# Chunked attention into a swish layer: compact q and k, 64x64 products, v in 128-token rows, stores from ScalarE's queue

## The chip, the cores and the metric

The kernel runs on one core of one Trainium2 chip. The metric is the device time of one execution in microseconds (us); lower is better. All medians and ratios below are of fast runs; a run over 1.5% above the fastest of its kernel counts as slow and is left out. The profile is a trace of one execution, with its own span (the kernel before: 403.8 us).

A core has five engines here, each with its own in-order stream of instructions: TensorE (PE in the profile; PEld are its weight loads), ScalarE (ACT), VectorE (DVE), GpSimd (POOL) and SyncE (SP), which only starts DMAs. A name with a trailing q (SPq, ACTq) is an engine's sequencer at work on issuing a DMA. An issue by ScalarE stands in ScalarE's own stream, between its computations.

## The reference, cut to what matters

```python
# q, k, v: (B=8, H=8, S=576, D=64); softmax only within chunks of 64 tokens
scores = 0.125 * q_chunk @ k_chunk.T          # 64 x 64 for each head and chunk
attn   = exp(scores - max) / sum
x      = (attn @ v_chunk)  -> (B*S = 4608 tokens, H*D = 512)
h      = x @ w_in                             # (4608, 512) @ (512, 2048)
g      = h * sigmoid(beta * h)
out    = g @ w_out                            # (4608, 2048) @ (2048, 512), float32
```

All inputs and the output are float32; the kernels compute in bfloat16. The sigmoid is done as a tanh: g is (tanh(beta h / 2) + 1) * h, and the factor 0.5 is applied when the result is stored. The maximum is left out of the softmax, and the sum comes from a column of ones beside v.

## The kernel before

The tokens are worked in nine blocks of 512. Blocks 0 to 7 are the first 512 tokens of each batch. Block 8 ("LAST") holds the 64 tokens that are left of each of the eight batches, so its q and k come in 32 DMAs of 64 KB instead of 8 of 256 KB. A block has two halves `h` of 256 tokens.

The program is a list of events with planned times. They are sorted by time and each is appended to the streams of its engines; semaphores are placed by a helper. The planned time has no other meaning than this order. From block 3 on, TensorE alternates a group of four 512-column products of the first layer (`mm1`, block b) with one of the second layer (`mm2`, block b-1), and the attention of block b+1 is strewn between them:

```python
        def load_v(blk, hb, halves, queue):          # 8 issues a block, 64 partitions each
            ...
                        a = v[blk][4 * hb + hp, 64 * c0:64 * c1, :].rearrange("(c k) d -> k c d", k=64)
            ...
                    return e.dma_start(vstage[64 * hb:64 * hb + 64, s, hp, c0:c1, :], a)

        def widen_k(h, hb, eng):                     # k into block-diagonal form, on GpSimd
            ...
                copy(eng, kBD[r, s, hp, :, 64 * hb:64 * hb + 64].rearrange("k c (t i) -> k c t i", t=8),
                     qkT[r, s, 1, :, :].rearrange("k i (c t h) -> k h c t i", c=4, h=4)[:, hp], ...)

        def gate(blk, t, n, halves=(0, 1)):          # tanh on ScalarE, g on VectorE
            ...

        def store(blk, s, n, cols=(0, 512), eng="act", queues=("sp", "sp")):
            ...                                      # evict PSUM on ScalarE, then two DMAs of 128 KB

        def rest(h, tc, tx, tk, t0, step, tX, tv):   # attention of half h
            for w in range(2):
                at(tc + 1.05 * w, cast_qk, h, w, "pool")
            at(tx, turn_dma, h)                      # DMA transpose of q and k, issued by SyncE
            for hb in range(2):
                at(tk + 2.0 * hb, widen_k, h, hb, "pool")
            at(tv, cast_v, h, "pool")
            for u in range(2):
                at(t0 + step * u, scores, ...)
                at(t0 + step * u + 0.3, exp, ...)
                at(t0 + step * (u + 1.5), attend, ...)
                at(t0 + step * (u + 1.5) + 0.3, normalize, ...)
            at(tX, turn_x_dma, h)                    # DMA transpose of x, issued by SyncE

        for blk in range(3, NB):
            b = begin(blk)
            for h in (2 * blk, 2 * blk + 1):
                for which in range(2):
                    at(b - 34, load_qk, h, which, "sp")
            for hb in range(2):
                at(b - 33.5, load_v, blk, hb, (0, 1), "sp")
            rest(2 * blk, b - 27, b - 24.5, b - 20.5, b - 15, 1.74, b - 9.5, b - 17)
            rest(2 * blk + 1, b - 24, b - 21.5, b - 15.5, b - 10, 1.74, b - 4.5, b - 12)
```

SyncE thus issues, in one order: q and k loads, v loads, the two q/k transposes, the two x transposes, and the stores in between. An issue whose data is not ready stops all that stand behind it.

## Time and profile before

| | kernel before |
|---|---|
| median of the three fast runs (range) | 402.83 us (401.52 to 405.39; a fourth, of 407.59, was slow) |
| span of the trace | 403.8 us |
| TensorE busy | 308.0 us (76%) |
| mean granted TensorE clock | 0.915 of full |

These are lines of the page of the kernel before. The rows of digits cut the span into 40 slices of about 10 us: a digit is the busy share in tenths, and in the row PEclk the granted clock. The line of the chain gives shares of the span by engine. The groups give line, engine, operation, shapes and count, then busy us, mean ns of one, and idle time just before with what ended most of it.

```profile
PE 308.0 (76%) x2020; PEld 158.9 (39%) x2049; DVE 145.0 (36%) x257; ACT 168.8 (42%) x275; POOL 130.4 (32%) x191
...
PE   1688986895698896898489938993899305899996
...
PEclk9999998898889998999699968998899855999999
...
PE 47%; SPq 18%; DMA 13%; DVE 7%; POOL 5%; ACT 5%; issue 4%; POOLq 0%; ACTq 0%
...
L381 PE MATMUL A<-qkT,kBD 128*128 128x64 bf16 x224 | 18.7, 235 | 49.5 <-POOL kBD L215 49.5
```

No engine is full. In the row PE a hole comes back about every four slices from the twentieth on, and the clock drops in the same place. In the chain of work that ended last, SyncE's queue (SPq) and DMAs make up 31%. The scores' products on TensorE (the last line) waited 49.5 us in all for the widened k.

The time line of SyncE between two blocks shows why the widened k is late. Columns: start us, duration us, engine, line, operation, destination and source, number of issues.

```profile
172.54 1.23 SPq L445 DMA_TRANSPOSE xT<-xn  x1
173.82 1.27 SPq L259 DMA_DIRECT2D qkstage<-in_q_dram  x2
...
179.00 8.11 SPq L281 DMA_DIRECT2D vstage<-in_v_dram  x8
187.16 1.34 SPq L510 DMA_DIRECT2D out_dram<-ostage  x2
188.54 3.32 SPq L347 DMA_TRANSPOSE qkT<-qkb  x1
...
193.17 3.15 SPq L347 DMA_TRANSPOSE qkT<-qkb  x1
...
213.63 1.23 SPq L445 DMA_TRANSPOSE xT<-xn  x1
```

And this is TensorE in that stretch; the bracket tells how long it was idle before the line, and who released it:

```profile
189.53 1.03 PE L460 MATMUL F<-xT,w_in_bf 128*128 128x512 bf16 x4
196.49 0.39 PE L381 MATMUL A<-qkT,kBD 128*128 128x64 bf16 x4 [5.93 <-POOL kBD L215]
...
197.68 1.49 PE L491 MATMUL F<-w_out_bf,g 128*128 128x512 bf16 x3 [0.22 <-issue]
```

A block is a loop: the second x transpose of one block leaves (172.54), only then do the next block's q and k loads, its v loads (8.11 us) and a store go out, then the q/k transpose (188.54); GpSimd widens k, the scores start (196.49, 24 us after the x transpose), and 17 us later the next second x transpose leaves (213.63). Together that is 41 us. TensorE stood for 5.93 us, and its next products ran at about half speed (three in 1.49 us against 0.81 at the full clock).

### The profile page before, as it was taken

To read this page: it belongs to the slowest core of one execution; us is meant where nothing else is said; L and a number is where in the kernel's file an instruction comes from. 1 tells how busy PE (TensorE), PEld (TensorE's weight loads), DVE (VectorE), ACT (ScalarE), POOL (GpSimd) and SP (SyncE) were. 2 spreads that over 40 slices of the span, in tenths; PEclk is the share of its full clock that TensorE was granted. 3 is DMA by queue.
4 is the path that set the end of the run, shared out by engine and by line. 5 is a ranking of instruction groups with operands and counts; after the bars stand their busy time and mean duration, and the time that the engine had idled before them with its cause. 6 is when DMAs were issued, how large, how long until landed. Compare 5 with 4: busy or idle time off the path is not lost.

```text
span 403.8 us, 5337 instructions
## 1 busy us (share of the span) xinstructions
PE 308.0 (76%) x2020; PEld 158.9 (39%) x2049; DVE 145.0 (36%) x257; ACT 168.8 (42%) x275; POOL 130.4 (32%) x191
## 2 busy tenths in 40 slices
PE   1688986895698896898489938993899305899996
PEld 1553444562344332433244414441444102444444
DVE  5257424551127531543044403541254200444410
ACT  1656235564147452535254515442454202545421
POOL 2544342417760128222831364034601218200000
PEclk9999998898889998999699968998899855999999
DMA  9997997992822695179516970699053295130112
GB/s 195 312 341 289 291 254 171 211 191 67 155 54 54 195 189 111 42 230 171 130 32 200 194 148 2 164 222 165 23 93 94 94 177 117 26 80 26 52 54 78
DMA packets 102809, 57.51 MB, mean 142 GB/s; under 512 B 84208, under 2 KB 85504, under 8 KB 102784
## 3 DMA queue, kind: packets, MB, share of 16 engines
q1 hardware_dynamic: 100432, 56.51, 61.1%
q10 hardware_dynamic: 2352, 0.66, 0.9%
q8 instruction: 16, 0.26, 0.3%
q14 instruction: 9, 0.07, 0.1%
HBM read 36.71 MB, written 9.44 MB: 114 GB/s over the span
## 4 chain that ended last, share of the span: by engine, by line
PE 47%; SPq 18%; DMA 13%; DVE 7%; POOL 5%; ACT 5%; issue 4%; POOLq 0%; ACTq 0%
PE F L491 20%; PE F L460 17%; DMA qkT<-qkb 8%; SPq L281 7%; SPq L267 5%; POOL kBD L215 5%; SPq L259 4%; DVE g L478 4%; PE A L381 3%; ACT tt L475 3%; PE A L414 3%; DMA xT<-xn 3%; PE A L460 2%; DVE xn L429 2%; SPq L510 2%
## 5 line engine op out<-in xcount | busy, mean ns | idle before, releaser
L478 DVE SCALAR_TENSOR_TENSOR g<-tt,F 128x512 bf16<-128x512 bf16 (+1 forms) x148 | 92.3, 629 | 201.5 <-ACT tt L475 201.2
L460 PE MATMUL F<-xT,w_in_bf 128*128 128x512 bf16 (+1 forms) x608 | 142.2, 368 | 14.7 <-DMA xT<-xn 7.7
L491 PE MATMUL F<-w_out_bf,g 128*128 128x512 bf16 (+1 forms) x563 | 146.8, 390 | 2.9 <-issue 0.8
L475 ACT ACTIVATE tt<-F,beta_half 128x512 bf16<-128x512 f32 (+1 forms) x148 | 93.5, 641 | 117.7 <-PE F L460 116.6
L460 PEld LDWEIGHTS F<-xT,w_in_bf 128*128 128x128 bf16 x608 | 59.0, 102 | 71.7 <-issue 10.2
L215 POOL COPY kBD<-qkT 64x256 bf16<-64x256 bf16 x112 | 64.7, 619 | 64.2 <-DMA qkT<-qkb 63.0
L491 PEld LDWEIGHTS F<-w_out_bf,g 128*128 128x128 bf16 x592 | 57.9, 101 | 63.3 <-issue 6.6
L215 POOL CAST qkb<-qkstage 128x1024 bf16<-128x1024 f32 x32 | 33.1, 1039 | 125.0 <-DMA qkstage<-in_q_dram 86.6
L381 PE MATMUL A<-qkT,kBD 128*128 128x64 bf16 x224 | 18.7, 235 | 49.5 <-POOL kBD L215 49.5
L398 ACT ACTIVATE EBD<-A 64x512 bf16<-64x512 f32 x56 | 32.9, 587 | 55.9 <-PE A L381 55.2
L381 PEld LDWEIGHTS A<-qkT,kBD 128*128 128x128 bf16 x224 | 15.0, 115 | 60.0 <-POOL kBD L215 55.1
L209 ACT ACTIVATE ostage<-F 128x512 f32<-128x512 f32 (+1 forms) x36 | 21.3, 591 | 26.6 <-PE F L491 20.6
L429 DVE TENSOR_TENSOR xn<-A,R 128x512 bf16<-128x512 f32 x36 | 24.9, 691 | 1.2
L215 POOL CAST v_bf<-vstage 128x1024 bf16<-128x1024 f32 x18 | 18.7, 1036 | 12.9 <-DMA vstage<-in_v_dram 12.0
L414 PE MATMUL A<-v_bf,EBD 128*128 128x65 bf16 x224 | 12.2, 198 | 8.9 <-DVE xn L429 8.4
L414 PEld LDWEIGHTS A<-v_bf,EBD 128*128 128x128 bf16 x224 | 10.8, 101 | 18.3 <-DVE xn L429 12.6
L427 DVE RECIPROCAL R<-A 128x8 f32<-128x8 f32 x36 | 7.3, 202 | 26.1 <-PE A L414 25.7
L460 PE MATMUL A<-xT,w_in_bf 128*128 128x512 bf16 x48 | 11.2, 380 | 2.4 <-DVE w_in_bf L215 1.3
L325 PE MATMUL F<-ident,qkb 128*128 128x128 bf16 x32 | 4.2, 312 | 8.2 <-DVE qkb L215 6.3
L475 ACT ACTIVATE tt<-A,beta_half 128x512 bf16<-128x512 f32 x12 | 8.2, 687 | 4.2 <-PE A L460 4.2
L478 DVE SCALAR_TENSOR_TENSOR g<-tt,A 128x512 bf16<-128x512 bf16 x12 | 8.2, 686 | 2.9 <-ACT tt L475 2.9
L215 POOL CAST w_in_bf<-wstage 128x512 bf16<-128x512 f32 x12 | 7.0, 615 | 6.3 <-DMA wstage<-in_moe_w_in_dram 6.3
(40 smaller groups left out, 74.2 us busy)
## 6 DMA issues: line engine op xcount, KB each, us to landing
out_dram<-ostage SPq DMA_DIRECT2D x70, 128.0 KB
qkstage<-in_q_dram SPq DMA_DIRECT2D x32, 256.0 KB, 3.4
qkstage<-in_k_dram SPq DMA_DIRECT2D x32, 256.0 KB, 5.4
vstage<-in_v_dram SPq DMA_DIRECT2D x56, 128.0 KB, 4.2
wstage<-in_moe_w_out_dram SPq DMA_DIRECT2D x4, 1024.0 KB
wstage<-in_moe_w_in_dram SPq DMA_DIRECT2D x3, 1024.0 KB
vstage<-in_v_dram SPq DMA_DIRECT2D x24, 64.0 KB, 5.4
wstage<-in_moe_w_in_dram SPq DMA_DIRECT2D x2, 512.0 KB
```

Source lines behind the costliest of these rows:

```text
L209: P.op("act", lambda e: e.activation(dst, src, AF.Copy, **kw), reads, writes)
L215: P.op(eng, lambda e: e.tensor_copy(dst, src), reads, writes, rows)
L267: return e.dma_start(qkstage[32 * c:32 * c + 32, s, which, hb, :], src[4 * hv + c][heads, S - 64:S, :].rearrange("h (t i) d -> t h (i d)", ...
L281: return e.dma_start(vstage[64 * hb:64 * hb + 64, s, hp, c0:c1, :], a)
L381: return e.matmul(unit_out(n, i, 64, r).rearrange("k (i t) -> k i t", i=8), kk, q_of(h, r, c, hp))
L398: P.op("act", lambda e, r=r: e.activation(EBD[r, s, u, :, r.start:r.stop], bank(n)[r, :].rearrange("p (x q) -> p x q", q=64), AF.Exp, scal ...
L414: return e.matmul(unit_out(banks[hp2], c, 65, r), ee, v_bf[r, sv, 2 * u + hp2, 4 * hv + c, 0:65])
L429: P.op("dve", lambda e: e.tensor_tensor(xn[:, s, :, u, :].rearrange("p c (b d) -> p b c d", b=2), o[:, :, :, 0:64], R[:, u, :, :].unsqueez ...
L460: return e.matmul(bank(n)[:, 64 * c0:64 * c1].rearrange("p (c t) -> p c t", t=64), w_in_bf[:, kt, 128 * t:128 * t + 128], xT[:, sx, c0:c1, ...
L475: P.op("act", lambda e: e.activation(tt[:, T % 3, c], bank(n)[:, c], AF.Tanh, scale=beta_half[:, t:t + 1]), reads=[K("ps", n, v=("h", blk, ...
L478: P.op("dve", lambda e: e.scalar_tensor_tensor(g2[:, sg, t, c], tt[:, T % 3, c], 1.0, bank(n)[:, c], ALU.add, ALU.mult), reads=[K("ps", n, ...
L491: P.op("pe", lambda e, t=t: e.matmul(bank(n)[:, 0:b - a], g2[:, sg, t, 128 * s:128 * s + 128], w_out_bf[:, t, a:b], start=(t == 0), stop=( ...
```

## The change

The intent is to make attention cheaper on every engine beside TensorE and to shorten SyncE's queue. q and k are put in token order once by GpSimd ("order"), so that neither a block-diagonal k nor zeroes are needed; scores and attention times v become 64x64 products on the four quarter tiles of TensorE; exp is one instruction for a half; v is loaded with 128 tokens on the partitions, in 4 issues a block instead of 8, half of them behind the q/k transposes; ScalarE issues the stores; w_out is loaded in runs of 4 KB (and beta, w_in columns and stored rows are rearranged to fit); q and k have a fourth buffer.

```diff
-        NQ = 3
+        NQ = 4
...
-        def load_v(blk, hb, halves, queue):
...
+        def load_v(h, cp, queue):
+            blk, hv, s, n = h // 2, h % 2, h // 2 % 2, 2 * (h % 2) + cp
+            if blk < LAST:
+                def f(e):
+                    return e.dma_start(vstage[:, s, n, :, :], v[blk][:, 128 * n:128 * n + 128, :].rearrange(
+                        "h p d -> p h d"))
...
-        def widen_k(h, hb, eng):
+        def order(h, which, eng):
             s = h % 2
...
+            copy(eng, qkO[:, s, which, :, :].rearrange("k h (t i) -> k h t i", i=8),
+                 qkT[:, s, which, :, :].rearrange("k i (t h) -> k h t i", h=4),
+                 [K("qkT", s, which, v=h)], [K("qkO", s, which, v=h)])
...
+        def scores(h, us=(0, 1)):
             s = h % 2
+            for u in us:
+                for cp in range(2):
+                    for hp in (2 * u, 2 * u + 1):
+                        for c2 in range(2):
+                            for hb in range(2):
...
+                                    return e.matmul(
+                                        bank(hb)[64 * c2:64 * c2 + 64, 64 * i:64 * i + 64],
+                                        qkO[r, s, 1, hp, 64 * c:64 * c + 64],
+                                        qkO[r, s, 0, hp, 64 * c:64 * c + 64])
...
-        def store(blk, s, n, cols=(0, 512), eng="act", queues=("sp", "sp")):
+        def store(blk, s, n, cols=(0, 512), eng="act", queues=("act", "act")):
...
-        def rest(h, tc, tx, tk, t0, step, tX, tv):
+        def rest(h, tc, tt_, to, tv, ts, tx):
             for w in range(2):
-                at(tc + 1.05 * w, cast_qk, h, w, "pool")
...
+                at(tc + 1.0 * w, cast_qk, h, w, "pool")
+                at(to + 2.0 * w, order, h, w, "pool")
+            at(tt_, turn_dma, h)
+            for cp in range(2):
+                at(tv, cast_v, h, cp, "pool")
+            at(ts, scores, h)
+            at(ts + 0.3, exp, h)
+            at(ts + 1.75, attend, h)
             for u in range(2):
...
+                at(ts + 2.1 + 0.1 * u, normalize, h, u)
+            at(tx, turn_x_dma, h)
...
-                    at(b - 34, load_qk, h, which, "sp")
-            for hb in range(2):
-                at(b - 33.5, load_v, blk, hb, (0, 1), "sp")
...
+                    at(b - 31.7, load_qk, h, which, "sp")
+                for cp in range(2):
+                    at(b - (26, 15)[h % 2], load_v, h, cp, "sp")
```

## The prediction

> **What bounds it now.** Time line and chain of waits: from block 3 on, every 512-token block takes about 41 us (starts at 136, 176, 217, 258, 302, 359 us). TensorE needs about 30.5: 32 groups of four 512-column products at 0.86 us = 27.6, plus 2.9 of attention. The rest is one loop through SyncE's queue. A block's second x transpose leaves at 172.5; only then the next block's q/k loads (8 issues, 5.2 us), v loads (8 issues, 8.1 us, DMA engines saturated), stores, and the q/k transpose (issued 188.5, landed 193.4). GpSimd widens k from 193.5; TensorE's in-order scores wait until 196.5: 5.9 us idle. The next second x transpose comes 17 us later (213.6). After each gap groups of four take 1.71 us instead of 0.86, some 2 us more. The Trainium skill, "TensorE: Matmul & The Clock Gate", Part 1, says that about 3.4 us of idleness halves the clock; the trace agrees (PEclk 0.5). The last block has 32 q/k issues of 0.695 us (22 us): 20.8 us idle before its scores.
>
> **What the change does.**
> - v: 4 issues per block, not 8, still 256-byte runs; half of them now after the q/k transposes. About 4 us less ahead of the transpose.
> - Stores leave SyncE's queue (2.5 us per block on the loop) for ScalarE: two issues of 0.62 us behind each eviction; tanh slips about 1 us, which two banks nearly hide (up to 1 us per block). The skill, "DMA: Bandwidth & Descriptors", says another issuing engine only saves sequencer time; that is what is wanted.
> - GpSimd: 16 widening copies of 0.58 us become 4 ordering copies, estimated at 1.8 us each from the strided rate; 4.7 becomes 3.7 on the chain.
> - TensorE: per block 64 full-array attention products become 128 small ones; at 29 ns (slope of the early 64x64 groups) 3.7 us plus mode changes: 1 us dearer.
> - Exp: two instructions per block, not eight. Fourth q/k buffer and earlier slots: scores to x transpose in 7 us of TensorE time, not 10.5.
> - w_out: under 1 us.
>
> **On the critical path.** New loop estimate: from x transpose, +6 loads, +4 v, +5 transpose, +4 order, +8 to 9 to the next x transpose: 29 us, below TensorE's own 32 to 33 (27.6 + 4.1 + about 1.5 of short waits). So a block becomes TensorE-bound at about 33, not 41, without half-clock stretches; the last still waits about 12 us for its loads. Early: DMA engines stay saturated until about 85 us, so only about 17 us are gained before block 3 (starts about 119). 119 + 5x33 + 13 + 45 (last block and tail, unchanged) = 342.
>
> Predicted 343 us, 8 in 10 between 325 and 363. Faster by over 2%: 0.96; within 2%: 0.03; slower: 0.01.
>
> **What would show it.** Right: block starts 32 to 34 us apart in the time line; scores' wait on k's copies (49.5 us in the wait view) below 20, almost all before the last block; mean PEclk above 0.95; stores on ScalarE's queue; ordering copies 1.6 to 2.0 us. Wrong: scores waiting 4 us or more for ordering copies in each block, or PE at half clock.
>
> **What would make it wrong.** Order copies of 3 us or more; q/k transposes slowed by sharing DMA engines with stores and v; ScalarE's store issues holding tanh and so the two F banks; tile-mode changes or small products over 60 ns each; column-stride-2 weights loading slower than a 216 ns product hides.

## The result

The changed kernel took 361.66 us (median of four runs, 357.85 to 362.96) against 402.83 for the kernel before in the same set; its results are correct. The ratio is 0.8953, with a 95% interval of 0.8854 to 0.9053. Ratios here are the mean time of one kernel's fast runs over that of the other's in the same rounds, so they are not quite the ratio of the medians. The time was in the predicted range (325 to 363), at its upper end: 18.7 us above the central 343 and 1.3 us below the bound.

These are the lines of the changed kernel's page that answer to those shown above.

```profile
PE 291.3 (81%) x2466; PEld 142.1 (39%) x2498; DVE 141.2 (39%) x255; ACT 148.5 (41%) x230; POOL 122.6 (34%) x126
...
PE   1688977698696799999699969996999009899996
...
PEclk9999999899989999999789989998999757999999
...
PE 40%; DMA 16%; SPq 12%; DVE 12%; ACT 7%; POOL 5%; issue 3%; ACTq 3%; DVEq 0%
...
L213 POOL COPY qkO<-qkT 128x1024 bf16<-128x1024 bf16 x28 | 53.6, 1952 | 32.2 <-DMA qkT<-qkb 32.2
...
L370 PE MATMUL A<-qkO 64*64 64x64 bf16 x576 | 9.8, 208 | 34.2 <-POOL qkO L213 26.3
```

The holes of TensorE became narrower, SyncE's share of the chain fell from 18% to 12%, and the scores' wait for GpSimd from 49.5 to 26.3 us. VectorE's share of the chain rose from 7% to 12%, and ScalarE's sequencer appeared with 3%: a new wait. Three 2.6 to 2.8 us waits in front of the scores are left, each with the half clock behind it (three products in 1.44 to 1.49 us); the first of them:

```profile
175.71 0.64 PE L370 MATMUL A<-qkO 64*64 64x64 bf16 x32 [2.76 <-POOL qkO L213]
176.68 1.49 PE L477 MATMUL F<-w_out_bf,g 128*128 128x512 bf16 x3 [0.33 <-issue]
```

Where the 43.8 us between the two spans went is read from the starts of each block's first `mm1`:

| stretch of the trace | before, us | after, us | difference |
|---|---|---|---|
| start to block 3 | 135.7 | 126.8 | -8.9 |
| blocks 3 to 6 (four intervals) | 166.1 | 137.4 | -28.7 |
| block 7 to LAST | 56.9 | 50.9 | -6.0 |
| LAST and the tail | 45.2 | 45.0 | -0.2 |

The same loop in the changed kernel's SyncE queue, one block:

```profile
191.15 1.23 SPq L426 DMA_TRANSPOSE xT<-xn  x1
...
197.81 1.27 SPq L275 DMA_DIRECT2D vstage<-in_v_dram  x2
200.59 7.74 SPq L341 DMA_TRANSPOSE qkT<-qkb  x2
208.38 1.21 SPq L275 DMA_DIRECT2D vstage<-in_v_dram  x2
```

From the x transpose (191.15) to the scores (211.90) it is 20.7 us instead of 24.0: 9.4 until the q/k transpose is issued (200.59), 7.4 until GpSimd's first ordering copy can start (208.00), 3.9 for the copies. From the scores to the next second x transpose (issued at 226.16) it is 14.3 us instead of 17.1; the prediction had 8 to 9. Together that is 35.0 us, about the interval between blocks from 4 to 7 (36.1, 35.1 and 35.0 in the table below). A part of the five or six microseconds too many is in this stretch, from the second half's exp to its normalization. ACTq L496 are the stores' issues, L461 the tanh, L464 g, L407 and L409 the normalization:

```profile
220.35 1.01 ACT L379 ACTIVATE E<-A 128x1024 bf16<-128x1024 f32 x1
...
221.25 0.60 ACT L207 ACTIVATE ostage<-F 128x512 f32<-128x512 f32 x1
...
221.86 0.45 PE L395 MATMUL A<-v_bf,E 64*64 64x65 bf16 x32
221.88 1.12 ACTq L496 DMA_DIRECT2D out_dram<-ostage  x2
...
223.05 0.69 ACT L461 ACTIVATE tt<-F,beta_half 128x512 bf16<-128x512 f32 x1 [1.20 <-PE F L477]
...
223.77 0.69 DVE L464 SCALAR_TENSOR_TENSOR g<-tt,F 128x512 bf16<-128x512 bf16 x1 [2.60 <-ACT tt L461]
...
224.37 0.20 DVE L407 RECIPROCAL R<-A 128x8 f32<-128x8 f32 x1
```

The AV products (attention times v, L395) were done at 222.3. The normalization could have begun then, but stands behind a g in VectorE's stream. That g waits (2.60 us) for a tanh, and the tanh stands behind exp, the eviction and two store issues of 1.12 us together in ScalarE's stream. So the normalization, the x transpose and the whole of the next loop start 2 us later than AV would allow. The profile's note "<-PE F L477" at the tanh names the releaser by semaphores; the 1.12 us of the issue itself fill that gap.

### The profile page after: what moved, and what is told of

It reads as the page before. It is cut to its first block, busy times and chain, and to the rows that moved or that the text cites. A ratio compares the mean times of both kernels' runs of the same rounds, so it can differ in the third digit from the quotient of the medians.

```text
span 360.0 us, 6004 instructions
## 1 busy us (share of the span) xinstructions
PE 291.3 (81%) x2466; PEld 142.1 (39%) x2498; DVE 141.2 (39%) x255; ACT 148.5 (41%) x230; POOL 122.6 (34%) x126
## 3 DMA queue, kind: packets, MB, share of 16 engines
q10 hardware_dynamic: 7856, 9.84, 10.3%
## 4 chain that ended last, share of the span: by engine, by line
PE 40%; DMA 16%; SPq 12%; DVE 12%; ACT 7%; POOL 5%; issue 3%; ACTq 3%; DVEq 0%
PE F L477 19%; PE F L444 11%; DMA qkT<-qkb 10%; DVE g L464 6%; SPq L265 6%; SPq L257 6%; POOL qkO L213 5%; DVE xn L409 3%; DMA qkstage<-in_k_dram 3%; ACT tt L461 3%; PE F L448 3%; ACTq L496 3%; PE A L444 3%; ACT E L379 3%; PE A L370 2%
## 5 line engine op out<-in xcount | busy, mean ns | idle before, releaser
L464 DVE SCALAR_TENSOR_TENSOR g<-tt,F 128x512 bf16<-128x512 bf16 (+1 forms) x148 | 91.8, 628 | 166.7 <-ACT tt L461 165.6
L477 PE MATMUL F<-w_out_bf,g 128*128 128x512 bf16 (+1 forms) x560 | 142.0, 381 | 5.8 <-issue 2.2
L461 ACT ACTIVATE tt<-F,beta_half 128x512 bf16<-128x512 f32 (+1 forms) x148 | 93.5, 641 | 127.0 <-PE F L444 104.4
L444 PE MATMUL F<-xT,w_in_bf 128*128 128x512 bf16 x448 | 117.9, 390 | 9.8 <-DVE g L464 6.4
L477 PEld LDWEIGHTS F<-w_out_bf,g 128*128 128x128 bf16 x592 | 56.3, 99 | 65.3 <-issue 3.5
L444 PEld LDWEIGHTS F<-xT,w_in_bf 128*128 128x128 bf16 x448 | 42.9, 100 | 69.5 <-DVE g L464 15.8
L213 POOL COPY qkO<-qkT 128x1024 bf16<-128x1024 bf16 x28 | 53.6, 1952 | 32.2 <-DMA qkT<-qkb 32.2
L370 PE MATMUL A<-qkO 64*64 64x64 bf16 x576 | 9.8, 208 | 34.2 <-POOL qkO L213 26.3
L379 ACT ACTIVATE E<-A 128x1024 bf16<-128x1024 f32 (+1 forms) x22 | 19.0, 865 | 34.0 <-PE A L370 34.0
L213 POOL CAST v_bf<-vstage 128x512 bf16<-128x512 f32 x36 | 21.6, 619 | 14.4 <-DMA vstage<-in_v_dram 14.1
L448 PE MATMUL F<-xT,w_in_bf 128*128 128x256 bf16 x160 | 23.2, 301 | 3.1 <-DVE g L464 1.7
L409 DVE TENSOR_TENSOR xn<-A,R 128x512 bf16<-128x512 f32 x36 | 24.9, 692 | 1.2
L370 PEld LDWEIGHTS A<-qkO 64*64 64x64 bf16 x576 | 7.2, 119 | 42.3 <-POOL qkO L213 28.8
L407 DVE RECIPROCAL R<-A 128x8 f32<-128x8 f32 x36 | 7.2, 201 | 17.3 <-PE A L395 17.3
L395 PEld LDWEIGHTS A<-v_bf,E 64*64 64x64 bf16 x576 | 7.3, 119 | 11.6 <-ACT E L379 4.1
L395 PE MATMUL A<-v_bf,E 64*64 64x65 bf16 x576 | 9.8, 208 | 2.2 <-ACT E L379 2.2
L461 ACT ACTIVATE tt<-A,beta_half 128x512 bf16<-128x512 f32 x12 | 8.2, 687 | 3.3 <-PE A L444 3.3
```

The costliest lines, as they stand in the source:

```text
L213: P.op(eng, lambda e: e.tensor_copy(dst, src), reads, writes, rows)
L370: return e.matmul(bank(hb)[64 * c2:64 * c2 + 64, 64 * i:64 * i + 64], qkO[r, s, 1, hp, 64 * c:64 * c + 64], qkO[r, s, 0, hp, 64 * c:64 * c ...
L379: P.op("act", lambda e: e.activation(E[:, s, :, a:b, :].rearrange("p g i q -> p g (i q)"), A[:, 0:2, 64 * a:64 * b], AF.Exp, scale=0.125), ...
L409: P.op("dve", lambda e: e.tensor_tensor(xn[:, s, u, :, :, :].rearrange("p c k (h d) -> p c (k h) d", h=2), o[:, :, :, 0:64], R[:, 2 * u:2 ...
L444: return e.matmul(bank(n).rearrange("p (v c t) -> p v c t", v=2, c=4), w, xT[:, sx, :, u, :, 64 * hb:64 * hb + 64], start=(kt == 0), stop= ...
L448: return e.matmul(bank(n)[:, 256 * hv:256 * hv + 256].rearrange("p (c t) -> p c t", c=4), w, xT[:, sx, hv, u, :, 64 * hb:64 * hb + 64], st ...
```

## The experiments

Four questions were put. Theory Q: the gain is one of SyncE's queue order, v and the stores in front of the q/k transpose; its rival: the cheaper attention on the compute engines. Theory S: the change lost part of its gain to the store issues in ScalarE's stream, by way of the order g, normalization on VectorE. Theory D: two q/k transposes issued back to back slow each other. And a check of whether the rotation over the tiles matters. The letters come back in the expectations. All kernels below gave correct results, and all runs are compared with runs of the kernel before on the same chip in the same rounds (its medians there: 402.06 to 403.31 us). The changed kernel's own ratio, 0.8953, comes from its first set; the experiments' ratios are set against it through the kernel before.

Intervals between blocks, in us, from the starts of each block's first tanh in the trace:

| kernel | 2 to 3 | 3 to 4 | 4 to 5 | 5 to 6 | 6 to 7 | 7 to LAST |
|---|---|---|---|---|---|---|
| before | 24.4 | 40.0 | 41.1 | 42.9 | 42.0 | 56.9 |
| after | 27.0 | 31.5 | 36.1 | 35.1 | 35.0 | 50.6 |
| b_stores_act | 23.5 | 41.1 | 46.9 | 47.3 | 45.2 | 57.5 |
| b_v_after | 24.9 | 39.9 | 40.8 | 40.7 | 40.0 | 55.8 |
| b_v_after_stores_act | 29.2 | 42.2 | 42.1 | 42.1 | 44.0 | 52.7 |
| b_loads_early | 32.2 | 39.5 | 39.3 | 39.0 | 35.1 | 56.7 |
| a_stores_sp | 27.1 | 29.5 | 31.4 | 31.3 | 31.2 | 50.6 |
| a_norm_first | 27.5 | 31.2 | 31.8 | 33.9 | 30.8 | 47.6 |
| a_qkT_serial | 27.4 | 31.6 | 34.0 | 34.9 | 34.7 | 50.3 |
| a_tile_runs | 26.9 | 31.6 | 33.2 | 35.0 | 33.9 | 50.7 |
| sp_v_front | 26.5 | 31.4 | 33.1 | 36.1 | 34.6 | 54.0 |
| sp_v_front_halves | 27.7 | 33.6 | 37.2 | 35.8 | 36.5 | 54.2 |
| a_sp_last | 27.0 | 29.6 | 31.3 | 35.6 | 38.7 | 30.2 |
| norm_all_early | 26.4 | 31.4 | 30.7 | 30.7 | 31.8 | 31.3 |

Kernels with b_ are the kernel before with an edit, the others are the changed kernel with one.

### b_stores_act: the kernel before, ScalarE issues its stores

```diff
-        def store(blk, s, n, cols=(0, 512), eng="act", queues=("sp", "sp")):
+        def store(blk, s, n, cols=(0, 512), eng="act", queues=("act", "act")):
```

> The kernel before, with only its stores moved to ScalarE's queue. Theory Q (SyncE's in-order queue is a loop: x transpose, loads, stores, q/k transpose, scores, x transpose): one store (1.3 us) stands ahead of each q/k transpose and one between the two, so a block gets 1.3 to 2.5 us shorter, and the 4.7 us wait for a store at 58 us goes: 10 to 20 us in all, 383 to 393 us. Rival P (the gain of the change comes from the cheaper attention on TensorE and GpSimd, not from the queue): within 2% of before.

Measured: 414.02 us (three fast runs; one of 420.04 was slow), ratio 1.0288 (1.0222 to 1.0355). The part that was to free SyncE's queue made the kernel slower, so both expectations failed. The first fence is of SyncE and GpSimd, the second of ScalarE in the second half's attention:

```profile
185.10 9.38 SPq L347 DMA_TRANSPOSE qkT<-qkb  x2
194.31 4.66 POOL L215 COPY kBD<-qkT 64x256 bf16<-64x256 bf16 x8 [9.39 <-DMA qkT<-qkb]
```

```profile
210.32 1.26 ACTq L510 DMA_DIRECT2D out_dram<-ostage  x2
211.63 0.69 ACT L475 ACTIVATE tt<-F,beta_half 128x512 bf16<-128x512 f32 x1 [1.34 <-PE A L414]
```

The 1.26 us of issues stand between the eviction and the next tanh and exp, which are on the way to the x transpose. But that is the smaller part of the loss. From the scores to the next second x transpose it takes 18.3 to 18.9 us for blocks 5 to 7, against 17.1 to 18.1 before. The larger part is that GpSimd can start on k only 9.2 us after the issue of the q/k transpose (185.10 to 194.31), against 5.0 in the kernel before (188.54 to 193.49), so that TensorE waits 10.3 us for the scores, not 5.9; the next two blocks are alike (9.4 and 9.3, against 5.8 and 5.7). Why the transpose lands later when ScalarE issues the stores was not tested on this kernel.

### b_v_after and b_v_after_stores_act: the kernel before, v loaded behind the q/k transposes

```diff
-                at(b - 33.5, load_v, blk, hb, (0, 1), "sp")
+                at(b - 21.4, load_v, blk, hb, (0, 1), "sp")
```

The second kernel also has the edit of b_stores_act.

> The kernel before, with only the eight v loads of a block moved behind its two q/k transposes in SyncE's queue. Theory Q: the q/k transposes are issued about 8 us earlier, the 6 us idle time before the first scores of a block goes with the half-clock time after it, and a block takes 33 to 36 us, not 41: 365 to 380 us. Rival P: within 2% of before. If the v loads then come too late, the wait moves to the AV products and little is gained.

> Both queue edits on the kernel before, its attention unchanged. Theory Q: 350 to 372 us, most of the 42 us that the change gained. Rival P: above 390 us.

Measured: 395.58 us, ratio 0.9834 (0.9807 to 0.9862), and with the stores on ScalarE 404.44 us, ratio 1.0041 (0.9989 to 1.0092). Theory Q's numbers failed in both; the times lie in rival P's windows, and the last sentence of the first expectation is what happened. TensorE's time line of b_v_after:

```profile
196.51 0.60 PE L414 MATMUL A<-v_bf,EBD 128*128 128x65 bf16 x8 [5.63 <-POOL v_bf L215]
```

The wait of 5.93 us for k became one of 5.63 us for v in the same stretch. Eight v issues cost the loop nearly as much behind the transposes as ahead of them: Q, as first put, is not enough. And moving the stores cost 9 us once more.

### a_stores_sp: the changed kernel, SyncE issues its stores

```diff
-        def store(blk, s, n, cols=(0, 512), eng="act", queues=("act", "act")):
+        def store(blk, s, n, cols=(0, 512), eng="act", queues=("sp", "sp")):
```

> The changed kernel, with only its stores moved back to SyncE's queue. Theory Q alone: 1.3 to 2.5 us per block are back on the loop and the early wait for a store returns: 370 to 382 us. Rival S (in the changed kernel the two store issues of 1.1 us on ScalarE stand between the exp and the tanh that hold up the normalization, so they are themselves on the loop): the two effects cancel, within 2% of the changed kernel, and the time from the last AV product to the second x transpose falls from 4 to about 3 us.

Measured: 350.13 us, ratio 0.8698 (0.8651 to 0.8744), 11.5 us faster than the changed kernel. So the stores' move was a loss inside the change, and the time is outside both windows: rival S was right about the stretch that it named (from the last AV product to the second x transpose 2.8 us instead of 3.9), but it foresaw no net gain. Blocks 4 to 7 come every 31.3 us instead of 35. In the trace the second x transpose leaves at 187.55 and the scores start at 207.28 (19.7 us; 20.7 with the stores on ScalarE), and the next second x transpose leaves at 218.85, 11.6 us after the scores instead of 14.3. The 1 us ahead of the scores is again the q/k transpose: the first ordering copy starts 6.1 us after its issue here, against 7.4. TensorE's wait ahead of the scores:

```profile
207.28 0.45 PE L370 MATMUL A<-qkO 64*64 64x64 bf16 x32 [1.68 <-POOL qkO L213]
207.88 0.81 PE L477 MATMUL F<-w_out_bf,g 128*128 128x512 bf16 x3 [0.16 <-issue]
```

After 1.68 us of waiting the products still run at the full clock (0.81 us), after 2.76 us they did not (1.49). So here a wait shorter by 1 us also saves what the half clock cost. The length of the wait alone does not decide it: after 2.67 us in a_tile_runs (at 177.84) and 3.49 us in sp_v_front (at 180.41) three products also took 0.81 us.

### a_norm_first: the changed kernel, normalization ahead of one gate

The stores stay on ScalarE. In blocks 3 to 7 the gate of the one tile whose g stood ahead of the second half's normalizations is placed behind them in VectorE's stream; the order on TensorE, ScalarE and GpSimd is unchanged.

```diff
-                at(t, mm1_gate, blk, i, F0 + i % 2 if slow else (F0, F1, F2)[i % 3])
+                n = F0 + i % 2 if slow else (F0, F1, F2)[i % 3]
+                if blk + 1 < NB and blk > 2 and i == 12:
+                    at(t, mm1, blk, i, n)
+                    at(t + 0.6, gate, blk, i, n)
+                else:
+                    at(t, mm1_gate, blk, i, n)
```

> The changed kernel with its stores left on ScalarE; in blocks 3 to 7 one gate of the block (the thirteenth) is given out after the two normalizations instead of before them, so VectorE no longer waits with the normalization for the tanh that stands behind a store on ScalarE. Theory S (ScalarE's store issues are on the loop through tanh, gate, normalization, x transpose): from the first scores of a block to its second x transpose 14.3 us becomes about 12, blocks 4 to 7 take about 33 us, not 35: 350 to 355 us. Rival D (what hurts is that without stores between them the two q/k transposes are issued back to back and the first lands late): under 1%, 358 to 362 us.

Measured: 350.14 us, ratio 0.8689 (0.8641 to 0.8737): as fast as with the stores on SyncE, and in theory S's window. The stretch that was shown of the changed kernel, in this one:

```profile
219.30 0.45 PE L395 MATMUL A<-v_bf,E 64*64 64x65 bf16 x32
219.32 1.12 ACTq L496 DMA_DIRECT2D out_dram<-ostage  x2
...
219.70 0.21 DVE L407 RECIPROCAL R<-A 128x8 f32<-128x8 f32 x1 [1.09 <-PE A L395]
...
220.49 0.69 ACT L461 ACTIVATE tt<-F,beta_half 128x512 bf16<-128x512 f32 x1 [1.20 <-PE F L477]
...
221.39 0.68 DVE L464 SCALAR_TENSOR_TENSOR g<-tt,F 128x512 bf16<-128x512 bf16 x1
```

The store issues still take 1.12 us and the tanh still comes after them. But the normalization starts at once with AV (219.70, against 2.5 us after AV's start before), and g comes last. Most of what the stores' move cost was therefore not ScalarE's 1.12 us as such, but an instruction of the loop that stood behind it on a third engine. The later landing of the q/k transpose is still there (7.4 to 8.4 us for blocks 5 to 7), and the two remedies were not run together.

### a_qkT_serial: the second q/k transpose waits for the first

```diff
-                reads=[K("qkb", s, w, v=h) for w in range(2)],
+                reads=[K("qkb", s, w, v=h) for w in range(2)]
+                + ([K("qkT", 0, 0, v=h - 1)] if s else []),
```

> The changed kernel with its stores left on ScalarE; the second q/k transpose of a block waits until the first has landed. Theory D: the first transpose lands within 5.5 us of its issue instead of 7.4, the first scores come 2 us earlier, blocks 4 to 7 take about 33 us: 350 to 355 us. Under theory S alone: 359 to 364 us. If both hold, this and the run before each give about half of the 11 us that moving the stores back gave.

Measured: 357.63 us, ratio 0.8866 (0.8807 to 0.8926), about 1% under the changed kernel with overlapping intervals: inconclusive in time. But the first transpose, now alone, still landed 7.2 us after its issue (199.87 to 207.10), so that the two slow each other is not supported. Why it takes 7 us with ScalarE's stores, and about 6 with SyncE's, stays open.

### a_tile_runs: four products of one tile in a row

The loops of `scores` and `attend` over the tiles are put outside, those over chunks and heads inside.

```diff
-                for cp in range(2):
-                    for hp in (2 * u, 2 * u + 1):
-                        for c2 in range(2):
-                            for hb in range(2):
+                for c2 in range(2):
+                    for hb in range(2):
+                        for cp in range(2):
+                            for hp in (2 * u, 2 * u + 1):
```

> The changed kernel with the order of the small attention products turned: all eight of one PE tile in a row, then the next tile, instead of the four tiles in rotation. In the changed kernel 32 products occupy TensorE for 0.38 us, 12 ns each. If that comes from four tiles working side by side, a run on one tile costs at least 27 ns each[...] and its weight loads show: 0.9 to 2 us per group of 32, four groups per block, so 2 to 6 us per block, of which waits on other engines may hide part: 365 to 400 us. If the four tiles do not matter: within 1% of 361.

(The expectation speaks of eight in a row; the loop over `u` stays outermost, so there are four. Its 27 ns is an estimate: an eighth of the 216 ns between the starts of 512-column products in these traces.) Measured: 359.67 us, ratio 0.8896 (0.8847 to 0.8945): no difference from the changed kernel. Between the start of 32 such products and the start of the group behind them lie 0.42 us here and 0.38 in the changed kernel: 12 to 13 ns for one, in either order. Why they are so cheap stays open.

### sp_v_front and sp_v_front_halves: what v's place and v's issues are worth

Both start from a_stores_sp. The first puts all v loads of a block ahead of its q/k transposes; the second also cuts each into two of 64 partitions for blocks 3 to 7, so that there are again eight issues.

```diff
-                    at(b - (26, 15)[h % 2], load_v, h, cp, "sp")
+                    at(b - 26, load_v, h, cp, "sp")
```

```diff
-            if blk < LAST:
+            if 3 <= blk < LAST:
+                for g in range(2):
+                    def f(e, g=g):
+                        return e.dma_start(
+                            vstage[64 * g:64 * g + 64, s, n, :, :],
+                            v[blk][:, 128 * n + 64 * g:128 * n + 64 * g + 64, :].rearrange("h p d -> p h d"))
+                    P.dma(queue, f, writes=[K("v", s, n, g, v=h)])
+            elif blk < LAST:
```

> Base: the changed kernel with its stores on SyncE (350 us, blocks 31.3 us). Here all four v loads of blocks 3 to 8 stand ahead of the two q/k transposes, as all v did before the change; number and shape of the loads unchanged. Theory Q (what stands ahead of the transposes in SyncE's queue sets the block): two more issues of 0.65 us and their 3 to 4 us of DMA time come into the loop, blocks of 33 to 35 us: 360 to 370 us. If the place of v does not matter: within 1% of 350.

> As the run before, and each v load of blocks 3 to 7 cut into two of 64 partitions, so eight issues per block as before the change (0.65 to 1.0 us each then: 8.1 us). Theory N (it is the number of issues that made v dear): blocks 3 to 6 us longer than in the run before, 375 to 395 us. Theory B (the same 256-byte packets cost the same however they are issued): within 1% of the run before.

Measured: 367.72 us (0.914, 0.9099 to 0.9181) and 376.11 us (0.9358, 0.9293 to 0.9424), both in their windows (the second's blocks 3 to 6 grew by 2.0 us on the mean, though, not by 3 to 6). On this kernel half of the v loads moved ahead costs 17.6 us, and eight issues instead of four another 8.4 us:

```profile
199.73 5.11 SPq L275 DMA_DIRECT2D vstage<-in_v_dram  x4
```

```profile
207.89 6.04 SPq L276 DMA_DIRECT2D vstage<-in_v_dram  x8
```

The first line is of sp_v_front, the second of sp_v_front_halves, both of SyncE in one block. Two issues stand there in a_stores_sp, for 1.58 us; the four take 5.11 us and the eight 6.04 us, and that time lies on the loop. The Trainium skill, "DMA: Bandwidth & Descriptors", Rules for kernel authors, advises one transfer of 128 partitions instead of two on disjoint halves, as they share the same engines; these runs agree, with 8.4 us for the cut.

### b_loads_early: the kernel before, loads of blocks 4 to 7 ahead of the x transposes

```diff
-                    at(b - 34, load_qk, h, which, "sp")
+                    at(b - (41 if 3 < blk < LAST else 34), load_qk, h, which, "sp")
             for hb in range(2):
-                at(b - 33.5, load_v, blk, hb, (0, 1), "sp")
+                at(b - (40.5 if 3 < blk < LAST else 33.5), load_v, blk, hb, (0, 1), "sp")
```

> The kernel before (its attention, v layout and stores untouched), with the q/k and v loads of blocks 4 to 7 given out ahead of the first x transpose of the block before, in a wait of SyncE's queue. If the queue order alone made its blocks 41 us long (theory Q), blocks 4 to 7 become 32 to 35 us: 370 to 380 us, about what the changed kernel gained without touching the attention. If the compute parts of the change (ordering copies in place of widening, small products, one exp) carry a large part, blocks stay at 37 us or more: above 385 us.

Measured: 397.75 us, ratio 0.9851 (0.9787 to 0.9915), so the number is the one that the expectation gives to the compute parts. But the trace shows another queue wait instead of compute. The loads now hold the x transposes, and a store that waits for its eviction holds the second q/k transpose:

```profile
204.81 7.50 SPq L281 DMA_DIRECT2D vstage<-in_v_dram  x8
212.36 2.63 SPq L445 DMA_TRANSPOSE xT<-xn  x1
```

```profile
220.55 1.86 PE L460 MATMUL F<-xT,w_in_bf 128*128 128x512 bf16 x4 [4.50 <-DMA xT<-xn]
```

The first fence is SyncE, the second TensorE at the start of the block, now waiting for x. In none of the three places tried (here, in the kernel before and in b_v_after) did the eight v issues hold up nothing. The test does not tell the two theories apart.

### a_sp_last: LAST's loads spread over earlier gaps

From a_stores_sp, the 32 q and k loads of LAST go out in four groups of eight, one or two blocks earlier.

```diff
-                    at(b - 31.7, load_qk, h, which, "sp")
+                    at(b - ((70, 65.6, 41.2, 36.8)[2 * (h % 2) + which] if blk == LAST else 31.7), load_qk, h, which, "sp")
```

> Stores back on SyncE, and the last block's 32 q/k loads given out one to two blocks earlier, eight at a time, in SyncE's waits for x (their staging buffers are free by then). Theory Q: the 19 us idle time before the last block's scores goes, the last block takes about 33 us instead of 50.6, and up to 5 us are lost where 8 loads overfill a wait: 331 to 338 us. If the loads hold up x transposes and stores instead: 340 us or more.

Measured: 342.21 us, ratio 0.8492 (0.8437 to 0.8548), 8 us faster than a_stores_sp, but not in Q's window: it is in that of loads that hold up x transposes. The last interval fell from 50.6 to 30.2 us; the two blocks that carry the loads grew to 35.6 and 38.7, since the loads stood ahead of x transposes:

```profile
263.22 1.87 PE L444 MATMUL F<-xT,w_in_bf 128*128 128x512 bf16 x4 [6.23 <-DMA xT<-xn]
```

### norm_all_early: a version that beats both

The changed kernel, with a_norm_first's edit, the q and k loads of blocks 4 to 7 issued while SyncE waits for the first x transpose of the block before, and LAST's in four groups spread over such waits and one place behind an x transpose. (The expectation's "two blocks earlier" is a slip: the planned time is 41 before the block's begin, against 31.7 in the changed kernel.)

```diff
-                    at(b - 31.7, load_qk, h, which, "sp")
+                    at(b - ((65.6, 60.4, 41.2, 36.8)[2 * (h % 2) + which] if blk == LAST else 41 if blk > 3 else 31.7), load_qk, h, which, "sp")
```

> The combination that the runs point to: stores on ScalarE, normalization ahead of the gate (350 us), q/k loads of blocks 4 to 7 given out in SyncE's wait for the first x transpose of two blocks earlier, and the last block's 32 loads spread over three waits and one place after an x transpose. Theory Q: the loads leave the loop, blocks 4 to 7 take 30 to 31.5 us instead of 32, the last interval about 31 instead of 47.6: 328 to 334 us. If the early loads hold back x transposes as they did when stores shared the queue: 340 us or more.

Measured: 327.57 us (327.23 to 328.66), ratio 0.8149 (0.8114 to 0.8184), a shade better than expected and 34 us better than the changed kernel. Its page, and then its SyncE around one block change:

```profile
PE 282.9 (87%) x2466; PEld 139.8 (43%) x2498; DVE 141.6 (43%) x255; ACT 147.1 (45%) x230; POOL 122.8 (38%) x126
...
PE   0688997579877677999999999989998999999996
...
PEclk9999999979997999999999999999999999999999
```

```profile
168.27 1.25 SPq L257 DMA_DIRECT2D qkstage<-in_k_dram  x2
178.12 6.62 SPq L426 DMA_TRANSPOSE xT<-xn  x2
184.79 1.26 SPq L275 DMA_DIRECT2D vstage<-in_v_dram  x2
186.09 7.45 SPq L341 DMA_TRANSPOSE qkT<-qkb  x2
```

The q and k loads now fill the time that SyncE would have waited before 178.12, and between the x transposes and the q/k transposes stand only 1.26 us of v. From block 3 on the holes of TensorE and of its clock are gone, and a block takes 30.7 to 31.8 us, which is about TensorE's own time for it: 32 groups of 0.86 us are 27.6, and the small products and their gaps make up most of the rest. Two of LAST's four groups still stand a little in the way: the second x transposes at 216.12 and 248.46 leave as these loads end, 1.9 and 2.8 us after their data was normalized.

## Why the prediction was right, and where its sum was off

- **The bound before** was named rightly: one loop through SyncE's queue of 24 + 17 us, with half clock after its gaps. The runs that broke the loop (norm_all_early) have neither the holes nor the half clock.
- **X transpose to scores** was predicted as 6 + 4 + 5 + 4, a little under 20 us; it measured 20.7. The term that was too small is the transpose: 7.2 to 7.6 us for blocks 4 to 7 from its issue to the first ordering copy, where 5 was predicted. Loads and v together took 9.4 (6 + 4 predicted) and the copies 3.9 (4). One ordering copy took 1.952 us (1.8 predicted). v ahead of the transposes shrank from 8.1 us to 1.3.
- **Scores to the next x transpose** is the term of the sum that was mis-sized most: 8 to 9 us predicted, 14.2 to 15.4 measured for blocks 5 to 7. The step that failed is "tanh slips about 1 us, which two banks nearly hide (up to 1 us per block)". The two banks of F may hide a late tanh from TensorE, but not from the normalization, which stood behind the g of that tanh in VectorE's stream. a_norm_first changes only the order of g and normalization, and a_stores_sp only the issuing engine; each brings blocks 4 to 7 from about 35 us to about 31 to 34 and the whole from 361.7 to 350.1. So a block predicted to be TensorE-bound at 33 us remained bound by the loop at 35. Only a part of the excess is this order: with it mended the stretch still takes 10.6 to 12.0 us (a_norm_first) or 11.6 (a_stores_sp), so that some 2 to 3 us more than predicted lie in the work between the two halves' attention itself. That was not tested. A loop of 19.7 + 11.6 = 31.3 us is just what a_stores_sp shows per block.
- **Moving the stores** was predicted as a gain of 2.5 us a block on the loop. It was a loss in both kernels: about 12 us on the kernel before, 11.5 us on the changed one. The prediction named the rival that holds tanh, and also "q/k transposes slowed by sharing DMA engines with stores and v"; the traces show both a held tanh and slower transposes (the larger part on the kernel before), but whether sharing is what slows them was not tested.
- **Small products** were predicted 1 us a block dearer. 32 of them take 0.38 us to the next group instead of 32 times 29 ns = 0.93 us, so that a block's 128 take 1.5 us at the full clock, against 2.9 for the 64 before (measured in the same way): 1.3 us cheaper.
- **Scores' wait** was predicted below 20 us, almost all before LAST; it is 26.3, of which 17.9 before LAST (12 predicted) and 2.6 to 2.8 in each of three blocks. The mean clock was 0.947 (above 0.95 predicted).
- **The sum**: block 3 starts at 126.8 (119 predicted, +7.8), four blocks take 137.4 (132, +5.4), the last interval 50.9 (46, +4.9), LAST and the tail 45.0 (45). Together 360.0 against 342; the terms are rounded. The errors of the sum all lie on one side, and the time stayed within the range by 1.3 us: the loop was the right mechanism, but that the range held is partly luck. The early part was also too hopeful. DMA engines were as full as predicted (a share of 1.04 of the stretch from 40 to 80 us), but block 2 took 27 us, not 25, and TensorE waited 3.19 us for x at its start.

What carries the 52 us between the kernel before (402) and a_stores_sp (350) is partly shown: on that kernel, putting all of v ahead of the transposes and back into eight issues gives back 26 us. The other half (the early part, which is 8.9 us in the changed kernel's trace, cheaper copies, products and exp, the fourth buffer, earlier places of the x transposes) was not taken apart, as these come together in one layout and one plan. That v's move or the loads' move alone brought 1.5% on the kernel before suggests that they pay only together with the fewer issues, which were not tried alone there; which of the compute parts they need stays open.

## What to carry to other kernels

A DMA issued by a compute engine takes its time in that engine's in-order stream; before moving stores there, look for the small instructions of the critical loop that stand behind them, also one engine further on, and at when the other queue's transfers land. When an in-order engine holds both work of the loop and work that only fills buffers, put the loop's first: moving one gate behind the normalizations in five blocks was worth 11 us here. Loads that wait for nothing belong in the queue's own waits, ended before the transfer that the loop needs, and in few large issues: here eight issues of 5 to 8 us held up something wherever they were put.

## What the Trainium skill lacked or had wrong

- "DMA: Bandwidth & Descriptors", Issuing engines are not separate DMA queues, says that issuing from another engine only saves sequencer time, usually small. It lacks the other side: the two issues of a store took 1.12 us of ScalarE's own stream (1.26 in b_stores_act), and moving the stores there cost 11.5 us in the changed kernel and about 12 us in the kernel before. In the latter the larger part came with a q/k transpose on SyncE's queue that took 9.2 us to the first copy, not 5.0; no run shows why.
- "TensorE: Matmul & The Clock Gate", Part 1, lets the clock halve after an idle window of about 3.4 us. In the changed kernel a wait of 2.76 us in the records was followed by half clock (three products in 1.49 us), one of 1.68 us in a_stores_sp and one of 3.49 us in sp_v_front were not (0.81 us). The ends of products in the profile are modelled, so the true idle time may differ.
- The same page, Part 1, gives about 25 ns as the least distance between the starts of two products, however small. 32 products of 64x64 on four tiles took 0.38 us to the next group, 12 ns each, and with four of one tile in a row 0.42 us, 13 ns each.
- No page that was read gives the time of the built-in GpSimd copy that rearranges bfloat16 ("GPSIMD Engine Reference" has costs per element of other kernels): 1.952 us for 128x1024 in the ordering copy, against 1.04 us for the cast of a float32 tile of that size.
